# Attention, gated MoE and routed MoE in one kernel: conversions, router and sums of weights placed anew around the last tile

## The chip, the cores and the metric

The kernel runs on one core of a Trainium2 chip. The core has five engines with instruction queues of their own: TensorE (PE, with its weight load shown as PEld), VectorE (DVE), ScalarE (ACT), GpSimd (POOL) and SyncE (SP, which here only issues DMAs). The metric is the device time of one execution in microseconds, the median of several runs.

## The reference

Three layers follow each other. The output of the first is the input of the second, and so on:

```python
scores = scale * np.matmul(q, k.transpose(0, 1, 3, 2))     # 2 batches, 8 heads, 576 x 64
kth = np.partition(scores, -top_k, axis=-1)[..., -top_k:-top_k + 1]   # top_k = 32
scores = np.where(scores >= kth, scores, -1e9)
...                                                        # softmax, times v
xn = x / rms * rms_g                                       # 1152 tokens, 512 wide
...
(silu(xn @ w_gate) * (xn @ w_val)) @ w_out                 # d_ff 1536
...
logits = x @ w_gate                                        # 8 experts
expert_idx = np.argmax(logits, axis=1)
...                                                        # slots of an expert in token order, at most 288
h = np.maximum(np.einsum('ecd,edf->ecf', disp, w1), 0.0)   # w1: 8 x 512 x 1024
y = np.einsum('ecf,efd->ecd', h, w2)                       # w2: 8 x 1024 x 512
out[i] = gate_w[i] * y[expert_idx[i], pos[i]]
```

## The kernel before

Tokens are worked on in nine tiles of 128. While the attention of a tile runs, the dense MoE (moe1) and the routing (dispatch) of tiles before it are mixed in. The last tile, number 8, has nothing left to be mixed with; its work and that of the routed MoE's first expert lie from about 490 us on, and it is there that the change edits.

moe1 of a tile computes, for three groups g of 512 columns, the gate and value products (L502), the gating on VectorE (th at L511, gs at L514), a transposition on PE (turned, L486) and its split into two float16 halves (L471). Then come 36 matmuls into one output (L531), which ACT copies to yx (L535). dispatch transposes yx (xu, L546), computes the 8 router logits (L558), copies them (lg, L561), scales the row to two float16 halves (yh on ACT at L573, yl on DVE at L574), finds the best expert (m8, key, k8, the one-hot oh at L595), counts the tokens before it with two small matmuls (L598, L599, result read by scr at L606), computes the slot (L619) and scatters the row to its expert's place in DRAM (disp, L621).

The routed MoE's sixteen weights (w1 and w2 of 8 experts) are float32 in DRAM. Each is loaded into a raw buffer (L779, two halves), its squares are summed on ACT (L795), the sums go over PE (L806) into a scale by a few VectorE operations of one column (L807 to L816, with the shared helpers at L148 and L151), and it is then split into float16 halves, "high" on ACT (L825) and DVE (L827), "low" on DVE (L830). Weight number n counts in the order of loading; weights 2 and 3 are those which the diff calls convert(2, 2) and convert(3, 3).

Each expert's matmuls take 168 slots. Expert 0 is divided: block "a" of 128 slots that earlier tiles have mostly filled, and block "b" of 48 gathered after the last scatter (rest_gather, L906 to L912, an indirect DMA to xb and a transposing DMA to xbT). up multiplies by w1 (L925, three matmuls per product: high by high, high by low, low by high), takes the ReLU (L936 on ACT, L937 on DVE, called hE); down multiplies by w2 and scales (L945); send transposes back (L966), scales (L973) and scatters rows to the output (L1007). finish does this for the last expert, in two parts, with the last 128 columns of the result transposed at L997 into two buffers named col.

The order on each engine is written by a scheduler, which takes the instructions' dependences, priorities (tc.high_priority) and explicit constraints: after(t, "x") puts what is in its block behind the instruction that was noted as behind[t, "x"]. Accumulators for up and down come from the pool pacc, which has three buffers of one PSUM bank.

## Time and profile before

| | us |
|---|---|
| median of 3 runs | 660.68 (660.37 to 664.24) |
| the profiled execution | 663.15 |
| its span | 661.2 |
| PE busy | 588.5 (89%) |
| DVE busy | 540.5 (82%) |
| ACT busy | 502.3 (76%) |
| POOL busy | 353.8 (54%) |

All times of rows are those of the span of the profiled execution, which counts from its first instruction. Busy time is that in which an engine works; a releaser is what ended an idle time.

### The profile page before, as it was taken

What the parts mean: (1) busy time and instruction counts of PE and PEld (TensorE: products, weight loads), DVE (VectorE), ACT (ScalarE), POOL (GpSimd) and SP (SyncE); (2) the same over time, 40 slices, a digit from 0 to 9 for tenths busy, and PEclk for the clock granted to TensorE, in tenths of its full rate; (3) what the DMA queues carried; (4) which work ended last, traced back from release to release, by engine and by line L of the source; (5) the groups of instructions that cost most, each with busy time, mean ns of one, the idle gap of its engine ahead of it and who ended that gap; (6) DMA issues with size and microseconds to landing.
All of it is one profiled execution on the core that took longest, in us unless ns stands there. A gap on an engine that the chain in (4) does not pass through costs nothing.

```text
span 661.2 us, 13479 instructions
## 1 busy us (share of the span) xinstructions
PE 588.5 (89%) x4817; PEld 412.1 (62%) x4817; DVE 540.5 (82%) x1495; ACT 502.3 (76%) x972; POOL 353.8 (54%) x490
## 2 busy tenths in 40 slices
PE   1418879799999999999999999999998888999995
PEld 1314455545666666666666666665544688999995
DVE  3989999978989979989988999871379756999961
ACT  3459978997787878878897988875697539999721
POOL 2486644646468879958788688583212200123212
PEclk9999979799999999999999999999999898999998
DMA  8998355923000010100000000007600499999001
GB/s 217 271 327 292 142 183 181 303 85 83 20 16 25 18 45 9 33 17 29 14 13 30 17 26 0 1 17 266 245 17 34 142 213 395 309 355 359 28 22 43
DMA packets 47008, 80.07 MB, mean 121 GB/s; under 512 B 18717, under 2 KB 23325, under 8 KB 46931
## 3 DMA queue, kind: packets, MB, share of 16 engines
q1 hardware_dynamic: 45138, 74.28, 35.7%
q0 software_dynamic: 1792, 4.83, 2.0%
q8 instruction: 40, 0.66, 0.4%
q14 instruction: 38, 0.30, 0.1%
HBM read 64.35 MB, written 12.27 MB: 116 GB/s over the span
## 4 chain that ended last, share of the span: by engine, by line
PE 52%; DVE 17%; ACT 9%; DMA 8%; POOL 6%; issue 6%; SPq 1%; POOLq 0%; DVEq 0%; ACTq 0%
PE pm L502 15%; PE pm L531 9%; PE acc L925 7%; PE xps L430 6%; PE tp L317 5%; PE tp L422 4%; DVE split L830 3%; DMA vt<-in_v_l_dram 3%; DMA raw<-in_w_dram 3%; ACT junk L795 2%; DVE r L373 2%; DVE wbig L169 2%; DVE wbig L168 2%; PE pm L486 2%; DVE split L827 2%
## 5 line engine op out<-in xcount | busy, mean ns | idle before, releaser
L502 PE MATMUL pm<-wbig,xn 128*128 128x512 f16 x600 | 145.7, 379 | 0.5 <-DVE hT L471 0.5
L925 PEld LDWEIGHTS <-split 128*128 128x128 f16 x1728 | 116.4, 99 | 4.3 <-issue 2.0
L399 POOL TENSOR_TENSOR pp<-s,pp 128x576 f32<-128x576 f32 x72 | 101.9, 1431 | 21.8 <-ACT pp L398 21.5
L502 PEld LDWEIGHTS <-xn 128*128 128x128 f16 x648 | 62.3, 98 | 60.2 <-issue 0.9
L376 DVE MAX8 m<-r 128x8 f32<-128x288 f32 x216 | 96.5, 452 | 2.5
L373 DVE MATCH_REPLACE8 r<-m,r 128x288 f32<-128x288 f32 x216 | 95.1, 442 | 0.0
L317 PE MATMUL tp<-kst,qh 128*128 128x288 f32 (+1 forms) x160 | 64.9, 413 | 31.9 <-ACT s L319 14.6
L531 PE MATMUL pm<-wbig,hT 128*128 128x512 f16 x324 | 78.4, 386 | 0.0
L830 DVE SCALAR_TENSOR_TENSOR split<-raw,sc,split 128x2048 f16<-128x2048 f32 (+1 forms) x32 | 65.9, 2077 | 0.5 <-ACT split L825 0.5
L319 ACT ACTIVATE s<-tp 128x288 f32<-128x288 f32 x144 | 56.7, 416 | 11.1 <-PE tp L317 9.5
L423 ACT ACTIVATE pt<-tp 128x384 f32<-128x384 f32 x108 | 51.8, 499 | 15.2 <-PE tp L422 10.6
L317 PEld LDWEIGHTS tp<-kst,qh 128*128 128x128 f32 (+1 forms) x160 | 31.4, 197 | 50.5 <-ACT s L319 20.7
L422 PE MATMUL tp<-ident,pp 128*128 128x128 f32 x324 | 57.8, 288 | 5.3 <-DVE r L325 2.5
L430 PE MATMUL xps<-pt,vt 128*64 128x128 f32 (+1 forms) x800 | 62.4, 275 | 0.0
L925 PE MATMUL acc<-hE,split 128*128 128x168 f16 (+2 forms) x864 | 59.9, 231 | 1.7 <-DVE hE L937 1.7
L795 ACT ACTIVATE junk<-raw 128x2048 bf16<-128x2048 f32 (+1 forms) x32 | 54.1, 1692 | 6.9 <-DMA raw<-in_w_dram 6.7
L398 ACT ACTIVATE pp<-s,bias 128x576 f32<-128x576 f32 x72 | 52.2, 777 | 9.4 <-POOL bias L381 9.3
L404 ACT ACTIVATE pp<-pp,bias 128x576 f32<-128x576 f32 x72 | 57.0, 792 | 2.3 <-POOL pp L399 2.1
L925 PE MATMUL acc<-xgT,split 128*128 128x168 f16 (+1 forms) x768 | 58.0, 239 | 0.0
L422 PEld LDWEIGHTS tp<-ident,pp 128*128 128x128 f32 x324 | 40.5, 145 | 23.8 <-ACT pt L423 3.8
L430 PEld LDWEIGHTS xps<-pt,vt 128*64 128x64 f32 x800 | 43.9, 139 | 13.7 <-issue 12.0
L531 PEld LDWEIGHTS <-hT 128*128 128x128 f16 x324 | 30.4, 99 | 33.5 <-issue 2.7
(241 smaller groups left out, 1227.7 us busy)
## 6 DMA issues: line engine op xcount, KB each, us to landing
raw<-in_w_dram SPq DMA_DIRECT2D x28, 1024.0 KB, 7.4
wbig<-in_w_gate_dram SPq DMA_DIRECT2D x6, 1024.0 KB, 8.5
wbig<-in_w_val_dram SPq DMA_DIRECT2D x6, 1024.0 KB, 8.3
wraw<-in_w_out_dram SPq DMA_DIRECT2D x12, 512.0 KB, 5.8
disp<-wraw SPq DMA_DIRECT2D x18, 257.0 KB, 6.5
qraw<-in_q_l_dram SPq DMA_DIRECT2D x72, 64.0 KB, 2.2
wbig<-in_k_l_dram SPq DMA_DIRECT2D x16, 288.0 KB, 4.4
split<-in_w_dram SPq DMA_DIRECT2D x4, 1024.0 KB, 9.3
```

Source lines behind the costliest of these rows:

```text
L317: nc.tensor.matmul(sp[:c1], x[:, i, :c1], kst[b, hp][:, i, c * HALF:(c + 1) * HALF], start=(n == 0), stop=(n == 1))
L373: nc.vector.match_replace(h[i], to[n - 1][:, i], h[i], -3.0e38)
L376: nc.vector.max(to[n][:, i], h[i])
L399: nc.gpsimd.tensor_tensor(w, s[i], w, op=OP.subtract)
L404: nc.scalar.activation(pp[p][:, i], pp[p][:, i], AF.Exp, bias=bias[:, i, 0:1], scale=0.125, accum_out=sums[t][:, h:h + 1])
L422: nc.tensor.transpose(tp[:, i, :], p2[:, o:o + P], ident)
L430: nc.tensor.matmul(xps[t][rows, hp, c0:c1], v, w, start=(n == 0), stop=(n == 4))
L502: behind[t, "prod", b] = nc.tensor.matmul(a, xn[:, x + c, :], half(i, lo), start=(c == 0 and n == 0), stop=(c == KC - 1 and n == 2))
L531: nc.tensor.matmul(yps, hT[f // KC][:, KC * hi + f % KC, :], half(i, lo), start=(f == 0 and n == 0), stop=(f == NF1 - 1 and n == 2))
L795: nc.scalar.activation(junk, raw[:, g * 2 * BIG // k:(g + 1) * 2 * BIG // k], AF.Square, accum_out=sc[:, 9 + g:10 + g])
L830: nc.vector.scalar_tensor_tensor(lo[:, r], raw[:, r], sc[:, 7:8], hi[:, r], op0=OP.mult, op1=OP.subtract)
L925: nc.tensor.matmul(a, u[:, c, col * P:(col + 1) * P], v[:, c, :a.shape[-1]], start=(c == 0 and n == 0), stop=(c == nk - 1 and n == 2))
```

## The change

There are five edits. The low halves of weights 1, 2 and 3 get other places among the gates, the transposed tiles and the slot of the last tile. The router of the last tile goes ahead of the first 24 matmuls of up "a", and the low half yl moves behind the one-hot. The squares of a weight (squares) become a function apart from its sums and scale (scales); for weights 5 and 6 the sums are called one step later, and the call of ready() between up 1 and down "b" moves behind up 2's. The raw buffers of weights from 4 on are taken in the order 0, 2, 3, 1. pacc gets a fourth buffer, and the last two transposes of finish share one buffer.

```diff
@@ -555,7 +555,7 @@
         yield
         lp = px.tile([P, 3, E], F32, name="px")
         for c in range(KC):
-            nc.tensor.matmul(lp[:, 0, :], yT[:, c, :], rg[:, c, :], start=(c == 0), stop=(c == KC - 1))
+            behind[t, "lp"] = nc.tensor.matmul(lp[:, 0, :], yT[:, c, :], rg[:, c, :], start=(c == 0), stop=(c == KC - 1))
         yield
         lg = route.tile([P, E], F32, name="lg")
         nc.vector.tensor_copy(lg, lp[:, 0, :])
@@ -571,7 +571,6 @@
         nc.vector.tensor_scalar(yn[:, 5:6], yn[:, 1:2], YS, None, op0=OP.mult)
         if t == NT - 1:
             nc.scalar.activation(yh, y, AF.Copy, scale=yn[:, 5:6])
-            nc.vector.scalar_tensor_tensor(yl, y, yn[:, 5:6], yh, op0=OP.mult, op1=OP.subtract)
         else:
             nc.scalar.activation(y, y, AF.Copy, scale=yn[:, 5:6])
             nc.scalar.activation(yh, y, AF.Copy)
@@ -592,8 +591,10 @@
         yield
         oh = route.tile([P, E], BF16, name="oh")
         ev = nc.vector if t == NT - 1 else nc.gpsimd
-        ev.tensor_scalar(oh, rank8, k8[:, 0:1], None, op0=OP.is_equal)
+        behind[t, "oh"] = ev.tensor_scalar(oh, rank8, k8[:, 0:1], None, op0=OP.is_equal)
         if t == NT - 1:
+            with after(t, "oh"):
+                nc.vector.scalar_tensor_tensor(yl, y, yn[:, 5:6], yh, op0=OP.mult, op1=OP.subtract)
             nc.tensor.matmul(lp[:, 2, :], ones16, cum, start=True, stop=True)
         nc.tensor.matmul(lp[:, 1, :], before, oh, start=True, stop=False)
         behind[t, "pe"] = nc.tensor.matmul(lp[:, 1, :], ones16, cum, start=False, stop=True)
@@ -603,7 +604,7 @@
         ev.tensor_scalar(pos[:, 1:2], k8[:, 0:1], -float(cap), float(cap * E), op0=OP.mult, op1=OP.add)
         nc.vector.tensor_scalar(nm[:, 2:3], nm[:, 1:2], EPSD, None, op0=OP.add)
         yield
-        nc.vector.scalar_tensor_tensor(scr, lp[:, 1, :], 1.0, oh, op0=OP.mult, op1=OP.mult, accum_out=pos[:, 0:1])
+        behind[t, "scr"] = nc.vector.scalar_tensor_tensor(scr, lp[:, 1, :], 1.0, oh, op0=OP.mult, op1=OP.mult, accum_out=pos[:, 0:1])
         nc.vector.reciprocal(nm[:, 3:4], nm[:, 2:3])
         yield
         ev.tensor_scalar(pos[:, 2:3], pos[:, 0:1], float(cap), NOWHERE, op0=OP.is_ge, op1=OP.mult)
@@ -768,7 +769,7 @@
 
         if n < 2:
             return slots[2 + n]
-        return raws[n % 2 if n < 4 else n % 4]
+        return raws[n % 2 if n < 4 else (0, 2, 3, 1)[n % 4]]
 
     def load(j, n):
         e, w = divmod(j, 2)
@@ -782,8 +783,11 @@
     BIG = 4 * DM
 
     def size(j, n):
-
-        e, w = divmod(j, 2)
+        squares(j, n)
+        scales(j, n)
+
+    def squares(j, n):
+
         raw = raw_of(n)
         sc = ew.tile([P, 13], F32, name="sc", bufs=8)
         k = 4 if n < 4 or exact else 2
@@ -793,9 +797,11 @@
             else:
                 junk = ew.tile([P, BIG], BF16, name="junk")[:, :2 * BIG // k]
             nc.scalar.activation(junk, raw[:, g * 2 * BIG // k:(g + 1) * 2 * BIG // k], AF.Square, accum_out=sc[:, 9 + g:10 + g])
+        sized[j] = sc
+
+    def scales(j, n):
         with tc.high_priority(offset=4000) if n < 4 and not exact else nullcontext():
-            scale(e, w, n, k, sc)
-        sized[j] = sc
+            scale(*divmod(j, 2), n, 4 if n < 4 or exact else 2, sized[j])
 
     def scale(e, w, n, k, sc):
 
@@ -882,18 +888,20 @@
     with after(NT - 1, "xn"):
         convert(1, 1, True, (0, 1))
     with after(NT - 1, "gs", 0):
-        convert(1, 1, False, (2, 3))
-    with after(NT - 1, "th", 1), after(NT - 1, "tanh", 1):
+        convert(1, 1, False, (2,))
+    with after(NT - 1, "gs", 1):
+        convert(1, 1, False, (3,))
+    with after(NT - 1, "th", 2), after(NT - 1, "tanh", 1):
         convert(2, 2, True, ())
-    with after(NT - 1, "gs", 1):
+    with after(NT - 1, "gs", 2), after(NT - 2, "scr"):
         convert(2, 2, False, (0, 1))
     with after(NT - 1, "dve"):
         convert(2, 2, False, (2, 3))
     fetch_w()
     size(3, 3)
-    pacc = ctx.enter_context(tc.tile_pool(name="pacc", bufs=3, space=PSUM, reuse_waits="tile"))
+    pacc = ctx.enter_context(tc.tile_pool(name="pacc", bufs=4, space=PSUM, reuse_waits="tile"))
     pback = ctx.enter_context(tc.tile_pool(name="pback", bufs=2, space=PSUM, reuse_waits="tile"))
-    ptp = ctx.enter_context(tc.tile_pool(name="ptp", bufs=2, space=PSUM, side="right", reuse_waits="tile"))
+    ptp = ctx.enter_context(tc.tile_pool(name="ptp", bufs=1, space=PSUM, side="right", reuse_waits="tile"))
     held = []
     if not exact:
         held.append(tc.alloc_tile_pool(name="held", bufs=1, side="right"))
@@ -930,11 +938,11 @@
         for lo, hi in groups(NF2, n):
             a = pacc.tile([P, hi - lo, n], F32, name="acc")
             for c in range(lo, hi):
-                with nullcontext() if early is None or c < early else after(NT - 1, "pe"):
+                with nullcontext() if early is None else after(NT - 1, "lp" if c < early else "pe"):
                     product(a[:, c - lo, :], place(2 * e), (xgT[k][:, :KC], xgT[k][:, KC:]), KC, F2, c)
             hh, hl = (x[:, lo:hi, :] for x in hE[k])
             nc.scalar.activation(hh, a, AF.Relu)
-            nc.vector.scalar_tensor_tensor(hl, a, 0.0, hh, op0=OP.max, op1=OP.subtract)
+            behind[k, "up"] = nc.vector.scalar_tensor_tensor(hl, a, 0.0, hh, op0=OP.max, op1=OP.subtract)
 
     def down(k, e, n):
         yT2[k] = eb.tile([P, KC, n], F32, name="yT2", bufs=1)
@@ -992,8 +1000,9 @@
         with tc.issue_after(last.ins):
             product(z[:, 0, :], place(2 * k + 1), hE[k], NF2, DM, x, range(cut, NF2))
         nc.vector.tensor_scalar(y[:, x:, :], z, es[k][:, 8:9], None, op0=OP.mult)
+        cols = ptp.tile([P, 2, P], F32, name="col")
         for i, (o, m) in enumerate(chunks(W)):
-            tp = ptp.tile([P, P], F32, name="col")
+            tp = cols[:, i, :]
             nc.tensor.transpose(tp[:m], y[:, x, o:o + m], ident)
             scaled(i, held[1 + i][1][:, x * P:], tp[:m], meta[k, i][:m, 0:1])
 
@@ -1012,9 +1021,11 @@
 
     up("a", 0, WA, 2)
     with after(NT - 1, "dve"), after(NT - 1, "tanh", 2):
-        convert(3, 3, True, (0, 1))
+        convert(3, 3, True, (0,))
     with after(NT - 1, "slot"), after(NT - 1, "gate"):
-        convert(3, 3, False, (2, 3))
+        convert(3, 3, False, (1, 2))
+    with after("a", "up"):
+        convert(3, 3, False, (3,))
     last = gather(1, 1, 0, W, eb, nc.sync)
     rest_gather()
     notes(1, 1, 0, W, eb, nc.sync)
@@ -1034,8 +1045,10 @@
         if n == 4:
             with after(NT - 1, "act"):
                 size(ORDER[4], 4)
+        if 5 <= n <= 6:
+            scales(ORDER[n], n)
         if n + 1 < 2 * E:
-            size(ORDER[n + 1], n + 1)
+            (squares if n < 6 else size)(ORDER[n + 1], n + 1)
         convert(ORDER[n], n)
         fetch_w()
 
@@ -1044,7 +1057,6 @@
     ready()
     send("a", WA, True)
     up(1, 1, W)
-    ready()
     down("b", 0, WB)
     ready()
     cnt = pback.tile([P, DM], F32, name="back")
@@ -1064,6 +1076,8 @@
         up(e, e, W)
         if done[0] < 2 * E - 1:
             ready()
+            if e == 2:
+                ready()
         if e == 2:
             send("b", WB, True)
         else:
```

Three places in the order show what the scheduler makes of it. Names carry the number of their tile; split2 and split3 are the destinations of weights 2 and 3, raw0 the raw buffer of weight 2.

VectorE, around the last tile's gate of group 2 (gs_6141, of th_6099), before:

```order
L511 SCALAR_TENSOR_TENSOR th_6099<-th_6099,late_6100 128x512
L830 SCALAR_TENSOR_TENSOR split2_5991<-raw0_5993,sc_6304,split2_5991 128x1024 x2
L514 SCALAR_TENSOR_TENSOR gs_6141<-late_6128,st_79,th_6099 128x512
L471 TENSOR_TENSOR hT_6006<-pm_6104,hT_6006 128x512
L604 TENSOR_SCALAR nm_6024<-nm_6024 128x1
L807 TENSOR_SCALAR sc_6342<-st_5988 128x1
L606 SCALAR_TENSOR_TENSOR scr_6069,pos_6068<-px_5961,oh_6047 128x8
L607 RECIPROCAL nm_6024<-nm_6024 128x1
L809 TENSOR_SCALAR sc_6342<-sc_6342 128x1
L810 TENSOR_SCALAR sc_6342<-sc_6342 128x1
L148 TENSOR_SCALAR sc_6342<-sc_6342 128x1
```

and now:

```order
L471 TENSOR_TENSOR hT_6006<-pm_6104,hT_6006 128x512
L514 SCALAR_TENSOR_TENSOR gs_6141<-late_6128,st_79,th_6099 128x512
L605 TENSOR_SCALAR nm_6024<-nm_6024 128x1
L813 TENSOR_SCALAR sc_6342<-st_5988 128x1
L607 SCALAR_TENSOR_TENSOR scr_6069,pos_6068<-px_5961,oh_6047 128x8
L836 SCALAR_TENSOR_TENSOR split2_5991<-raw0_5993,sc_6304,split2_5991 128x1024 x2
L608 RECIPROCAL nm_6024<-nm_6024 128x1
L815 TENSOR_SCALAR sc_6342<-sc_6342 128x1
L471 TENSOR_TENSOR hT_6007<-pm_6150,hT_6007 128x512
L836 SCALAR_TENSOR_TENSOR split2_5991<-raw0_5993,sc_6304,split2_5991 128x1024 x2
L816 TENSOR_SCALAR sc_6342<-sc_6342 128x1
L148 TENSOR_SCALAR sc_6342<-sc_6342 128x1
```

The two low halves of weight 2 (L830, now L836) stand behind the gate rather than ahead of it, and the exponent of weight 3 (the rows of sc_6342, ending in L148) comes behind four low halves.

PE, from the sums of weight 4 (st_5988) in down "a" (acc_6516, operands hE0 and hE1), before:

```order
L806 LDWEIGHTS ones16_70
L806 MATMUL st_5988<-s16_6720,ones16_70 128x1 [waits DVE_49]
L806 LDWEIGHTS ones16_70
L806 MATMUL st_5988<-s16_6720,ones16_70 128x1
L925 LDWEIGHTS split1_5990
L925 MATMUL acc_6516<-hE0_6381,split1_5990 128x128 [waits Activation_49]
L925 LDWEIGHTS split1_5990
L925 MATMUL acc_6516<-hE1_6382,split1_5990 128x128 [waits DVE_49]
```

and now:

```order
L812 LDWEIGHTS ones16_70
L812 MATMUL st_5988<-s16_6720,ones16_70 128x1
L812 LDWEIGHTS ones16_70
L812 MATMUL st_5988<-s16_6720,ones16_70 128x1
L933 LDWEIGHTS split1_5990
L933 MATMUL acc_6516<-hE0_6381,split1_5990 128x128 [waits Activation_49]
L933 LDWEIGHTS split0_5989
L933 MATMUL acc_6616<-xbT_6499,split0_5989 128x48 [waits DMAHW6_49]
```

One matmul of down "a" follows the sums in both; then the products of up "b" (xbT_6499) come, of which the first waits for a DMA, and the other 83 of down "a" stand behind 42 of them.

PE, its last matmuls, which end in the two transposes to col (yT2_8574 is the result to be transposed), before:

```order
L925 LDWEIGHTS split0_5989
L925 MATMUL acc_8576<-hE0_8326,split0_5989 128x168
L997 MATMUL col_8691<-ident_64,yT2_8574 128x128 [waits DVE_49]
L997 MATMUL col_8694<-ident_64,yT2_8574 40x128
L1076 TENSOR_LOAD top_7017 [waits DVE_49]
L53 COMPARE_AND_BRANCH
```

and now:

```order
L933 LDWEIGHTS split0_5989
L933 MATMUL acc_8576<-hE0_8326,split0_5989 128x168
L1006 MATMUL col_8691<-ident_64,yT2_8574 128x128 [waits DVE_49]
L1006 MATMUL col_8691<-ident_64,yT2_8574 40x128 [waits Activation_49]
L1090 TENSOR_LOAD top_6987 [waits DVE_49]
L53 COMPARE_AND_BRANCH
```

The second transpose goes to the same tile as the first and waits for ACT, which reads that one.

## Rows read from the trace of the kernel before

**Rows 1.** Stretches of the span: start:end, length, busy us (instructions), clock, DMA share, GB/s.
```profile
510.75:513.50 2.75, 2.75 (x8) 0.91 (x6) 2.55 (x10) 2.70 (x3) 2.13 (x4) 0.50 0.87 354
...
536.05:537.74 1.69, 0.01 (x2) 0.01 (x1) 1.69 (x1) 0.00 (x0) 0.00 (x0) 1.00 0.49 102
551.30:554.36 3.06, 3.06 (x86) 3.06 (x83) 2.99 (x13) 3.06 (x4) 0.00 (x0) 0.53 1.03 420
554.36:620.99 66.63, 66.63 (x918) 66.32 (x915) 64.00 (x110) 62.83 (x68) 13.81 (x7) 1.00 0.94 302
```

**Rows 2.** Timeline of DVE: start, duration, operation, tile, [idle before, its releaser].
```profile
506.86 2.46 DVE L830 SCALAR_TENSOR_TENSOR split<-raw,sc,split 128x1024 f16<-128x1024 f32 x2
509.25 0.73 DVE L514 SCALAR_TENSOR_TENSOR gs<-late,st,th 128x512 f32<-128x512 f32 x1
...
511.14 0.15 DVE L148 TENSOR_SCALAR sc<-sc 128x1 int32<-128x1 int32 x1
...
524.74 0.27 DVE L619 TENSOR_SCALAR slot<-pos 128x1 int32<-128x1 f32 x1
...
625.64 4.60 DVE L830 SCALAR_TENSOR_TENSOR split<-raw,sc,split 128x2048 f16<-128x2048 f32 x2
...
654.65 0.34 DVE L1002 TENSOR_SCALAR last<-col,notes 40x128 f32<-40x128 f32 x1 [0.54 <-PE col L997]
```

**Rows 3.** Timeline of PE, columns as in rows 2.
```profile
510.04 0.72 PE L486 MATMUL pm<-ident,gs 128*128 128x128 f32 x4 [1.82 <-DVE gs L514]
...
520.13 1.50 PE L925 MATMUL acc<-xgT,split 128*128 128x128 f16 x24
521.47 1.01 PE L558 MATMUL px<-rg,xu 128*128 128x8 f32 x8
...
531.26 4.79 PE L925 MATMUL acc<-hE,split 128*128 128x128 f16 x83 [0.51 <-DVE hE L937]
537.74 2.60 PE L925 MATMUL acc<-xbT,split 128*128 128x48 f16 x96 [1.68 <-DMA xbT<-xb]
...
549.87 0.19 PE L806 MATMUL st<-s,ones 128*128 128x1 bf16 x2 [2.94 <-DVE s L804]
...
550.86 3.67 PE L925 MATMUL acc<-hE,split 128*128 128x48 f16 x96
...
623.25 7.12 PE L925 MATMUL acc<-hE,split 128*128 128x168 f16 x96 [1.23 <-DVE hE L937]
630.21 7.12 PE L925 MATMUL acc<-xgT,split 128*128 128x168 f16 x96
...
654.17 0.44 PE L997 MATMUL col<-ident,yT 128*128 128x128 f32 x2 [0.49 <-DVE yT L994]
```

**Rows 4.** The chain of waits: start, duration, engine and line.
```profile
510.76 8.11 PE pm L531 x30
...
518.89 0.70 ACT yx L535
...
522.18 0.75 DVE yd L574
```

**Rows 5.** Timeline of ACT, columns as in rows 2.
```profile
511.32 2.19 ACT L825 ACTIVATE split<-raw,sc 128x1024 f16<-128x1024 f32 x2
...
520.33 0.60 ACT L546 ACTIVATE xu<-px 128x512 f32<-128x512 f32 x1
...
654.54 0.37 ACT L1004 ACTIVATE last<-col,notes 128x128 f32<-128x128 f32 x1 [1.22 <-PE col L997]
```

**Rows 6.** Timeline of POOL, columns as in rows 2.
```profile
525.88 1.27 POOL L621 DMA_INDIRECT disp<-yd,slot  x1 [1.40 <-DVE slot L619]
...
657.01 0.93 POOL L1007 DMA_INDIRECT out_dram<-last,to  x1 [0.31 <-issue]
```

**Rows 7.** Timeline of SP's DMA queue, columns as in rows 2.
```profile
518.18 0.38 SPq L779 DMA_DIRECT2D raw<-in_w_dram  x1
```

**Rows 8.** DMA issues of the page: line, count, KB each, median us to landing.
```profile
raw<-in_w_dram SPq DMA_DIRECT2D x28, 1024.0 KB, 7.4
```


## The prediction

> **What bounds the kernel now.** The page's busy shares put PE first, but they are an average, so I read stretches. The table of stretches shows the routed experts from 554.36 to 620.99: PE busy 66.63 of 66.63 us, DVE 64.00, ACT 62.83, DMA engines at 0.94 [rows 1]. All four are nearly full there; only an earlier start, or fewer stops of PE, shortens that stage. The two views that follow, the chain of waits and the timelines, are read for how this start comes about. In the chain, the last tile of the dense MoE runs from VectorE's gating into the transposes, the 30 output products, ACT's yx, and the router with its long row of small VectorE operations [rows 2 to 5]; it ends in the slot number and the last scatter of tokens [rows 6]. From that scatter hang the gather of block "b", its transposition and 96 products at 537.74, which waited 1.68 us for it [rows 3]. Thirdly PE's own stops: 2.94 us at 549.87 (sums of a weight's squares), 1.23 us before 623.25 [rows 3].
>
> **The last tile: VectorE's low halves.** Two low halves of weight 2, 2.46 us, stand before the gate of group 2 and now follow it [rows 2]. This is on the chain: the gate starts at 509.25 and PE, after 1.82 us of idling, turns its result at 510.04 [rows 2, 3]. So the turn comes 2.46 us earlier. The products behind it ran at a granted clock of 0.50 for 2.75 us from 510.75 [rows 1]; less idling ahead of them may leave the clock at 1.00, which saves half of that, 1.4 us (bounds 0 and 1.4). I take it, since the low half moved out of PE's preceding wait as well; the products, 8.11 us in the chain [rows 4], would end 3.9 us earlier.
>
> ACT does not allow that whole gain. Its pair of conversions of weight 3 (2.19 us at 511.32 [rows 5]) stands ahead of yx in its order and waits for an exponent that VectorE wrote at 511.14 [rows 2]. That write now comes behind four low halves (twice 2.46 us [rows 2]) and a halving of a transposed tile: gate at 506.8, its end at 507.5, plus 4.9, plus some 1.3 of small operations (0.15 each, as the exponent itself) and one of about the gate's 0.73: 513.7. ACT's pair then ends at 515.9, and yx, at 518.89 before [rows 4], starts there: 3.0 us earlier. This replaces the 3.9.
>
> **The router.** The 24 early products of "a" started at 520.13 and lasted 1.50 us; the transposed row was ready at 520.33 + 0.60 = 520.93, yet the router started at 521.47 [rows 3, 5]. With the router ahead it saves 0.54. The logits' copy then waited for VectorE's low half of y, 0.75 us at 522.18 [rows 4], till 522.93, with the router done at 521.47 + 1.01 = 522.48 [rows 3]: 0.45 more. This low half now stands between the one-hot and the slot: 0.75 back. The 24 products come after instead; they delay "a", which has idle time behind it. Sum to the slot (524.74) and the scatter (525.88) [rows 2, 6]: -3.0 - 0.54 - 0.45 + 0.75 = **-3.2 us**. Ends: -2.3, if the clock's part fails, and -4.4, if ACT's pair is ready early.
>
> **PE behind the scatter.** Before, 83 products of down "a", 4.79 us at 531.26, ran while "b" was on its way [rows 3]. The scheduler now puts 42 products of up "b" ahead of them, and the first of these waits for the transposing DMA, as the order shows. Everything behind it on PE waits too: the 83 products, the rest of up "b", up 1. So the 4.79 us move from under the wait to behind it. PE then idles for about 6 us (528.5 to 534.5) rather than 1.68. What the clock does then is bounded by rows: after the 1.69 us stretch 536.05 to 537.74 it stayed at 1.00, and after the 2.94 us stop it fell to 0.53 for 3.06 us [rows 1, 3]. I take 1.4 us lost (half of 2.75), with ends 0 and 2.8. The stop of 2.94 us goes, because the sums' matmuls now stand behind down "b", where VectorE's inputs are long there. With it goes the half clock in down "b": 96 products took 3.67 us there, and the same number and shape in up "b" 2.60 [rows 3]; 1.07 off. Sum: +4.79 + 1.4 - 1.07 - 2.94 = **+2.2 us**.
>
> On the clock, the trace has both cases, no drop after 1.69 us and a drop after 2.94. The Trainium skill, "TensorE: Matmul & The Clock Gate", section "What's actually happening", says that the throttled state is the default and that activity releases it; by this the long wait would surely cost a slow start, and the sum would keep its 1.4. Were the short stop's row to decide, the sum would be 1.4 lower. The 2.94 us row is nearer to a 6 us wait, and by it the page's rule holds here.
>
> **The fourth accumulator.** The 1.23 us ahead of 623.25 were spent waiting for VectorE's hE to free one of three buffers [rows 3]; a fourth takes it away: **-1.23**, ends -1.23 and 0. What would be late next is weight 14: its last two low halves, 4.60 us from 625.64, end at 630.24, just as PE began up 7 at 630.21 [rows 2, 3]. They must come earlier too; the loads' start moves with the scatter, and VectorE has 2.63 us of idle time in the stage [rows 1].
>
> **The last columns.** Two transposes took 0.44 us together at 654.17 [rows 3]. They now share a buffer, and the second waits for ACT's copy, 0.37 us at 654.54 [rows 5]; this delays VectorE's scaling at 654.65 by about 0.5 [rows 2]. But the store that needs it went out at 657.01, 2.0 us after that scaling ended, behind the store before it [rows 2, 6]. So 0; if that cover were gone, up to 0.8.
>
> **The rest at nothing.** Squares are computed apart from sums, in ACT's queue, which has 3.8 us of room over the stage; the raw buffers change places in the loads' order, under DMA at 0.94 [rows 1]. On SP the second half of weight 4 now goes ahead of the gather of "a" and its notes, where it was issued at 518.18 after them [rows 7]; that is a rival's ground.
>
> **Sum.** -3.2 + 2.2 - 1.23 + 0 = -2.2 us (-3.2 + 2.18 - 1.23 = -2.25). The profiled execution took 663.15 us, 2.5 over the median of 660.68; the sum is taken off the median: **658.4 us**. Its ends: -4.4 + 0.78 - 1.23 = -4.85, or 655.8; and -2.3 + 3.58 + 0 + 0.8 = +2.1, or 662.8.
>
> **Rivals.**
> *Full gain.* PE's clock does not fall after the long wait, and ACT's pair does not hold yx. For it: the 1.69 us row; against it: the 2.94 us one. It gives 655.8. A step further, "b" arrives before PE has run out of work, and the 4.79 and 1.4 fall away too, leaving -1.07 - 2.94 = -4.0 behind the scatter: 660.68 - 4.4 - 4.0 - 1.23 = 651.0; for that "b" would have to come 9 us earlier, and nothing in the rows speaks for it.
> *The scatter waits (slower side).* The last scatter writes rows that the gather of "a" and its notes must have read. A load of 1024 KB landed after 7.4 us in the median [rows 8], and the gather now queues behind one. With the load out at about 514 the gather could land at 523 or later, where the scatter is due at 522.7. From that point on each microsecond is lost; by 3.2 us later the whole gain of the tile is gone: 660.68 + 2.2 - 1.23 = 661.6, and with one more half-clock stretch of 1.4, 663.0. Against it: the transfers of 510.75 to 513.50 ran at 354 GB/s [rows 1], by which 1024 KB take 3.0 us.
> *VectorE holds the end.* Weight 14's low halves don't follow, since hE comes from a PE that is only 1.0 us earlier after the scatter. Then the stop at 623 turns into a wait at 630: 660.68 - 1.0 = 659.7.
> *Nothing.* PE's 83 products go behind the wait and eat all of the tile's gain, and weight 14 holds the rest: 660.7, at the edge of the last.
>
> **Chances.** Forecast 0.5, full gain 0.15, scatter 0.17, VectorE or nothing 0.18. The forecast's own range is 655.8 to 662.8; 655.3 to 663.0 leaves out the tails of the first two rivals, and some 0.2 in all. One per cent, 6.6 us, is about what a measurement of this kernel can tell from no change: faster means under 654.1, slower over 667.3. The first needs a full gain in which the wait for "b" costs nothing; the second more than one rival at once. Faster 0.10, same 0.85, slower 0.05.
>
> **What would show it.** The gate of group 2 starts at about 506.8, yx at 516, the slot at 521.5; PE idles some 6 us before the first product on xbT at 534.5, and the 83 products of down "a" follow it; no stop of 2.9 us before the sums, none of 1.2 us after up 6; the final store goes out when the one before it is issued. If yx comes at 515.0, ACT's wait was wrong; if the scatter starts over 1.5 us after its slot, the load was in the way; if PE stops before up 7, weight 14 holds it. The forecast falls if the slot comes less than 2 us earlier, or if PE does not idle before xbT.

## The result and the profile after

The changed kernel takes 667.42 us (median of 8 runs, 666.04 to 669.25); the kernel before, run beside it, 662.5 us (8 runs, 658.46 to 664.64). The ratio is 1.009 with a 95% interval of 1.0066 to 1.0115: **the change costs about 4.9 us, 0.9%**, where 658.4 us were forecast, 2.2 us under the time before, and above the stated range of 655.3 to 663.0. The prediction had put the border of "slower" at one per cent, or 667.3 us; the ratio lies just under it, the time just over it. The profiled execution took 666.40 us, with a span of 664.4 us.

The first 480 us are the same program, yet their length differs by execution. So times are also given from a marker: the start of the last tile's first transposes of the attention's output (L465), up to which the order is the same in all kernels here. It is at 478.63 in the trace before and at 477.30 in that after.

The stretches after; columns as in [rows 1]:

```profile
507.45:514.20 6.75, 6.64 (x32) 2.84 (x29) 6.68 (x12) 1.90 (x3) 4.47 (x4) 1.00 0.49 183
...
527.50:532.33 4.83, 0.00 (x1) 0.00 (x0) 4.66 (x9) 2.00 (x1) 0.00 (x0) 0.68 0.83 142
532.33:539.62 7.29, 7.29 (x125) 7.29 (x125) 3.47 (x2) 0.60 (x1) 0.00 (x0) 0.74 1.03 334
...
550.91:604.00 53.09, 53.09 (x735) 52.92 (x731) 50.24 (x92) 45.70 (x49) 6.57 (x5) 1.00 1.04 321
604.00:624.28 20.28, 15.63 (x196) 15.07 (x195) 16.14 (x28) 16.55 (x20) 1.92 (x2) 0.93 0.37 118
```

The 30 products of the last tile run at a clock of 1.00, where [rows 1] has 0.50 for 2.75 us. Then PE stands still from 527.50 to 532.33, and its clock is 0.74 in the 7.29 us behind. Up to 604.00 PE is full. In the next 20.28 us it works 15.63.

PE's timeline after; columns as in [rows 3]:

```profile
477.30 0.64 PE L465 MATMUL xps<-ident,x 128*128 128x128 f32 x4
...
506.96 0.66 PE L486 MATMUL pm<-ident,gs 128*128 128x128 f32 x4 [0.88 <-DVE nm L605]
507.45 6.64 PE L531 MATMUL pm<-wbig,hT 128*128 128x512 f16 x30
...
532.33 1.84 PE L933 MATMUL acc<-xbT,split 128*128 128x48 f16 x42 [4.84 <-DMA xbT<-xb]
533.99 5.79 PE L933 MATMUL acc<-hE,split 128*128 128x128 f16 x83
...
548.38 2.59 PE L933 MATMUL acc<-hE,split 128*128 128x48 f16 x96
550.81 0.19 PE L812 MATMUL st<-s,ones 128*128 128x1 bf16 x2
...
607.60 0.19 PE L812 MATMUL st<-s,ones 128*128 128x1 bf16 x2 [0.91 <-DVE s L810]
...
621.45 0.19 PE L812 MATMUL st<-s,ones 128*128 128x1 bf16 x2 [3.73 <-DVE s L810]
621.50 1.28 PE L933 MATMUL acc<-xgT,split 128*128 128x168 f16 x8
622.57 1.91 PE L974 MATMUL back<-ident,yT 128*128 128x128 f32 x8
624.28 7.41 PE L933 MATMUL acc<-hE,split 128*128 128x168 f16 x96
...
656.38 0.29 PE L1006 MATMUL col<-ident,yT 128*40 128x128 f32 x1 [0.46 <-ACT last L1013]
```

The row at 532.33 is the wait that the order showed, with the 83 products behind it. The 2.94 us stop ahead of down "b" [rows 3] is gone; the sums of weight 5 now come behind down "b", at 550.81. The 1.23 us stop of [rows 3] is gone too, but two others are there, 0.91 and 3.73 us, both at sums of squares, and the matmuls behind the longer one run slow (8 transposes 1.91 us; at 602.16 they took 1.04).

DVE's timeline; columns as in [rows 2]:

```profile
506.17 0.74 DVE L514 SCALAR_TENSOR_TENSOR gs<-late,st,th 128x512 f32<-128x512 f32 x1
...
512.71 0.15 DVE L148 TENSOR_SCALAR sc<-sc 128x1 int32<-128x1 int32 x1
...
520.69 0.26 DVE L620 TENSOR_SCALAR slot<-pos 128x1 int32<-128x1 f32 x1
...
552.48 1.28 DVE L833 TENSOR_SCALAR split<-raw,sc 128x2048 f16<-128x2048 f32 x1
...
605.06 2.34 DVE L836 SCALAR_TENSOR_TENSOR split<-raw,sc,split 128x2048 f16<-128x2048 f32 x1
...
621.22 0.17 DVE L810 CAST s<-sc 128x2 bf16<-128x2 f32 x1 [3.80 <-ACT junk L799]
```

ACT's timeline; columns as in [rows 5]:

```profile
512.90 2.19 ACT L831 ACTIVATE split<-raw,sc 128x1024 f16<-128x1024 f32 x2 [4.65 <-DVE sc L148]
514.99 0.67 ACT L535 ACTIVATE yx<-pm,st 128x512 f32<-128x512 f32 x1
...
539.02 1.91 ACT L799 ACTIVATE junk<-raw 128x2048 bf16<-128x2048 f32 x1 [7.21 <-DMA raw<-in_w_dram]
...
541.59 1.91 ACT L799 ACTIVATE junk<-raw 128x2048 bf16<-128x2048 f32 x1
...
617.15 1.91 ACT L799 ACTIVATE junk<-raw 128x2048 bf16<-128x2048 f32 x1 [3.69 <-SPq L53]
```

And the view of the raw buffers' instructions between 590 and 622 us (count, ns as min/median/max, first and last start; then the time from issue to landing):

```profile
L780 SPq DMA_DIRECT2D raw<-in_w_dram x5: 367/368/533, 591.0 to 607.4; - x5
...
DMA to landing us min/median/max: 9.6/9.6/9.6
```

The long stop can be followed back through these three. PE waits for DVE's cast at 621.22, that for ACT's squares, the last of which start at 617.15 and 619.19; their load was issued at 607.40, when DVE's low half that read the raw buffer had ended (605.06 + 2.34), and landed 9.6 us later. This is the last weight, number 15. The squares of weight 5, in contrast, were done at 543.5, and its conversion started only at 552.48, behind sums that PE did at 550.81.

POOL's last rows; columns as in [rows 6]:

```profile
521.81 1.26 POOL L622 DMA_INDIRECT disp<-yd,slot  x1 [1.57 <-ACT junk L799]
...
658.42 0.93 POOL L1016 DMA_INDIRECT out_dram<-last,to  x1 [0.30 <-issue]
```

The last store follows the one before it, so the wait between the two column transposes cost nothing.

### The profile page after: what moved, and what is told of

It reads as the page before. It is cut to its first block, busy times and chain, and to the rows that moved or that the text cites. A ratio compares the mean times of both kernels' runs of the same rounds, so it can differ in the third digit from the quotient of the medians.

```text
span 664.4 us, 13481 instructions
## 1 busy us (share of the span) xinstructions
PE 589.2 (89%) x4817; PEld 413.4 (62%) x4817; DVE 540.3 (81%) x1495; ACT 502.6 (76%) x972; POOL 353.7 (53%) x490
## 5 line engine op out<-in xcount | busy, mean ns | idle before, releaser
L531 PE MATMUL pm<-wbig,hT 128*128 128x512 f16 x324 | 76.6, 380 | 0.0
L836 DVE SCALAR_TENSOR_TENSOR split<-raw,sc,split 128x2048 f16<-128x2048 f32 (+1 forms) x32 | 65.8, 2077 | 0.1
L531 PEld LDWEIGHTS <-hT 128*128 128x128 f16 x324 | 30.2, 98 | 32.4 <-issue 0.9
```

The costliest lines, as they stand in the source:

```text
L531: nc.tensor.matmul(yps, hT[f // KC][:, KC * hi + f % KC, :], half(i, lo), start=(f == 0 and n == 0), stop=(f == NF1 - 1 and n == 2))
L836: nc.vector.scalar_tensor_tensor(lo[:, r], raw[:, r], sc[:, 7:8], hi[:, r], op0=OP.mult, op1=OP.subtract)
```

## The experiments

The change was taken apart, then one reason after the other was put to the test. In the tables, slot, xbT (the first product of "b"), up 2 and the last group (the last matmuls of down 7) are in us from the marker, read from one trace each. "Stops" are PE's from up 2 on.

| kernel | slot | xbT | up 2 | last group | stops | ratio to before (95%) |
|---|---|---|---|---|---|---|
| before | 46.1 | 59.1 | 75.7 | 174.2 | 1.23 | 1 |
| change | 43.4 | 55.0 | 73.6 | 177.0 | 0.91, 3.73 | 1.0090 (1.0066 to 1.0115) |
| e5, fourth buffer alone | 44.4 | 56.5 | 74.7 | 176.0 | 0.92, 3.36 | 1.0113 (1.0084 to 1.0143) |
| e3, change with three buffers | 45.0 | 57.6 | 70.1 | 173.7 | 3.40 | 1.0034 (1.0007 to 1.0060) |
| e1, change with sums back | 43.4 | 55.6 | 73.9 | 177.8 | 1.79, 3.35 | 1.0048 (1.0018 to 1.0077) |
| e4, last tile's edits alone | 45.3 | 57.7 | 71.5 | 172.8 | 1.82, 0.78, 1.25 | 1.0011 (0.9982 to 1.0040) |
| e8, change, "b" behind "a" | 43.4 | 56.8 | 69.1 | 173.3 | 0.27, 2.78, 0.35, 0.42 | 1.0005 (0.9981 to 1.0030) |
| e11, e8 with sums back | 43.4 | 56.5 | 75.8 | 172.5 | none | 0.9999 (0.9974 to 1.0025) |

**e3_three_acc** takes the fourth buffer out of the change:

```diff
-    pacc = ctx.enter_context(tc.tile_pool(name="pacc", bufs=4, ...
+    pacc = ctx.enter_context(tc.tile_pool(name="pacc", bufs=3, ...
-        cols = ptp.tile([P, 2, P], F32, name="col")
-            tp = cols[:, i, :]
+            tp = ptp.tile([P, P], F32, name="col")
```

> The change without its fourth accumulator and the shared column buffer (pacc 3, two column buffers). In the order the 83 products of down a stand ahead of those of up b again, and weights 8 and 9 are converted one after the other. Theory RING (the time is lost because the low halves of weights 8 and 9 are interleaved, which frees a raw buffer some 2.3 us late, so that the last weights' loads and sums come late and PE stops 3.7 us in up 6): that stop is gone, up 2 starts at about 545 to 546, and the kernel is 8 to 9 us faster than the changed one, about 3 us faster than the kernel before (ratio 0.995). Theory BOUND (loads and VectorE's conversions set the end whatever comes before up 2): up 2 starts as early, but PE stops elsewhere before up 7, and the time is that of the kernel before within 1 us. Theory PLACE (the 83 products behind the wait are the loss): the loss of 4.8 and of the slow clock goes, but a stop in up 6 of over 2 us stays.

**e5_four_acc_alone** makes the same edit the other way round in the kernel before.

> The kernel before with only the fourth accumulator and the shared column buffer. 32 products of up b now stand ahead of 83 of down a. Theory PLACE: PE waits some 7 us before the first product on xbT instead of 1.7, up 2 starts 4 to 5 us later than 554.4, and the end is 3 to 5 us later than before (the 1.2 us stop goes). Theory BOUND: the later start is absorbed since weights come no later, within 1 us of before. Theory RING: weights 8 and 9 are not interleaved, so no stop of 3.7 us in up 6; the time is PLACE's.

By itself the fourth buffer costs 1.13%, and without it the change is 0.56% better than with it (1.0034 and 1.0090, their intervals just apart): it is the edit that costs most. The interval of e3 lies above 1 too, so some 0.3% may belong to the other edits. With the buffer alone the scheduler already places 32 products of "b" ahead of 83 of down "a". PE's timeline of e5:

```profile
536.42 1.44 PE L925 MATMUL acc<-xbT,split 128*128 128x48 f16 x32 [3.66 <-DMA xbT<-xb]
537.68 5.62 PE L925 MATMUL acc<-hE,split 128*128 128x128 f16 x83
...
629.83 3.65 PE L925 MATMUL acc<-hE,split 128*128 128x168 f16 x48 [3.36 <-DVE hE L937]
```

The stop for hE, which the buffer was to take away, is there in another form, 48 products into the same product: hE is late because VectorE is.

**e1_sums_back** undoes the edits on sums and ready():

```diff
-        if 5 <= n <= 6:
-            scales(ORDER[n], n)
-            (squares if n < 6 else size)(ORDER[n + 1], n + 1)
+            size(ORDER[n + 1], n + 1)
...
+    ready()
     down("b", 0, WB)
...
-            if e == 2:
-                ready()
```

> The change with the sums of weights 5 and 6 and the calls of ready() put back. Weights 8 and 9 are converted one after the other; the 42 products of up b still stand ahead of the 83 of down a. Theory RING: the stop of 3.7 us in up 6 is gone, so the time is 3 to 5 us under the changed kernel's, about 663; a stop of up to 3 us for the sums of weight 5 is back before up 2. Theory BOUND: as the changed kernel within 1 us. Theory PLACE: as the changed kernel, the long wait before xbT unchanged at about 4.8 us.

Weight 5's conversion starts at 69.7 us from the marker, not 75.2, yet the last group comes at 177.8. The wait for xbT is 5.68 us here. The ratio's interval overlaps that of the change.

**e4_last_tile_alone** undoes that edit too, the buffers' order and the fourth buffer; what is left are the edits of the last tile.

> The kernel before with only the edits of the last tile (low halves, router, yl): raw buffers, sums and accumulators as before. PE order has the 83 products ahead of up b. Theory RING: slot 4 us earlier, up 2 at about 549 to 550, no interleaving, so 3 to 4 us faster than before (ratio 0.994 to 0.996). Theory BOUND: up 2 earlier by as much, but stops before up 7 make it the time of before within 1 us.

Up 2 starts 4.2 us earlier from the marker, the last group 1.4, and the time is the same within 0.4%. The earlier start is real; it does not arrive.

**e8_b_behind_a** is the change, all of it, with one constraint that puts up "b" behind down "a" again:

```diff
-                with nullcontext() if early is None else after(NT - 1, "lp" if c < early else "pe"):
+                with (after("a", "dpe") if k == "b" else nullcontext()) if early is None else after(...):
...
-                product(a[:, c - lo, :], place(2 * e + 1), hE[k], NF2, DM, c)
+                behind[k, "dpe"] = product(a[:, c - lo, :], place(2 * e + 1), hE[k], NF2, DM, c)
```

> The whole change, with one constraint more: the products of up b stand behind all products of down a on PE, as in the kernel before. Theory CONVERSIONS (from weight 5 on VectorE converts one weight after the other at about 8 us each, slower than PE uses them, so the end is set by when weight 5's conversion starts; in the change it waits for sums that stand behind down b on PE): the wait for xbT falls to about 2 us, up 2 starts 4 to 6 us earlier than in the change (counted from the last tile's first transposes), weight 5's conversion starts as much earlier, and the end comes 4 to 6 us earlier, at the kernel before or 1 us under it. Theory LATE STOP (the change's loss arises only behind up 2, from the late load of weight 15 and its sums ahead of up 6's last matmuls): the stop of 3.7 us stays or grows, the time is the changed kernel's within 1 us.

It is level with before (1.0005), and its interval lies wholly under that of the change: one constraint on PE's order takes the loss back, with the fourth buffer still there. It does not act on PE alone, though: from the conversion of weight 4 on, 31 of VectorE's 158 instructions stand in another order in e8's trace than in that of the change (in the two traces of the change, 2). PE's timeline of e8:

```profile
530.72 4.79 PE L933 MATMUL acc<-hE,split 128*128 128x128 f16 x83 [0.51 <-DVE hE L946]
535.72 2.58 PE L933 MATMUL acc<-xbT,split 128*128 128x48 f16 x96 [0.21 <-DMA xbT<-xb]
...
547.97 0.19 PE L812 MATMUL st<-s,ones 128*128 128x1 bf16 x2
...
561.79 0.19 PE L812 MATMUL st<-s,ones 128*128 128x1 bf16 x2 [2.78 <-DVE sc L813]
561.84 7.09 PE L933 MATMUL acc<-hE,split 128*128 128x168 f16 x56
```

The wait for xbT falls from 4.84 to 0.21 us, and the 83 products take 4.79 rather than 5.79. Up 2 starts 6.6 us before that of the kernel before. Behind it PE stops 2.78 us, 56 products then take 7.09 us where 96 take 7.12 at full clock, and of 6.6 us 0.9 are left.

**e11_b_behind_a_sums_back** is e8 and e1 together.

> As the run before it, and the sums of weights 5 and 6 and the calls of ready() put back too, so that the sums of weight 5 stand in up 1. CONVERSIONS: weight 5's conversion starts another 2 to 3 us earlier; the end comes at 3 us under the kernel before unless the order on VectorE puts hE behind a conversion, as it did in the change with the sums back (a stop of 3.4 us in down 6), which gives the time of before. LATE STOP: like the change with the sums back, 3 us over the kernel before.

PE never stops from up 2 on, but 5.12 us in up 1, for weight 5. PE, and ACT, in e11:

```profile
546.00 0.19 PE L812 MATMUL st<-s,ones 128*128 128x1 bf16 x2 [5.12 <-DVE s L810]
```

```profile
543.74 1.91 ACT L799 ACTIVATE junk<-raw 128x2048 bf16<-128x2048 f32 x1 [1.48 <-DMA raw<-in_w_dram]
```

ACT squares the second half of weight 5 as soon as the load lands, so here the stop hangs on a load; the DMA engines' share was 1.01 from 541 to 546 us. What the last tile gains, PE spends waiting for weight 5.

**e10_last_tile_raw_order** is e4 with the new order of the raw buffers, 1.0014 (0.9989 to 1.0038), against 1.0011 for e4: the order of the buffers alone is worth nothing that shows.

> The kernel before with the last tile's edits and the new order of raw buffers, three accumulators and the sums where they were. CONVERSIONS: against the last tile's edits alone the sums of weight 5 come some 1 to 2 us earlier where the loads do; the order puts them behind up 1, so weight 5's conversion starts when down b does, no earlier than about 71 us behind the last tile's first transposes; the end is within 1 us of that kernel's. LATE STOP: weight 15 is loaded into the buffer of weight 11, as in the change, so a stop of 2 to 4 us in up 6 appears.

**e9_extra_low_half** adds 2.34 us to VectorE in the kernel before, by computing one low half of weight 7 twice:

```diff
+            for _ in range(2 if n == 7 and g == 0 else 1):
                 nc.vector.scalar_tensor_tensor(lo[:, r], raw[:, r], ...
```

> The kernel before with one low half of weight 7 computed twice: 2.3 us more of VectorE's work, nothing else added. CONVERSIONS: weight 14's conversion, which PE waits for at up 7 with no slack, moves by 2.3 us and so does the end: 2 to 2.5 us slower than before. If PE sets the pace (weight 5 is ready 10 us ahead of its use), no change within 0.5 us.

1.0066 (1.0026 to 1.0106), that is 4.4 us (1.7 to 7.0): the interval holds the 2.34 us, so VectorE's time in the routed stage can be paid for at the end in full, and the middle is nearly twice that. In the trace up 2 starts at 75.4 us from the marker and the last group at 177.9, 3.7 later than before, with stops of 0.60, 0.45, 1.18 and 2.53 us, the last three for hE (that up 7 waits for weight 14, as expected here, is a wrong reading; the next section has it). The test is not clean: the second computation also holds weight 7's raw buffer longer, and from the conversion of weight 4 on the scheduler put 32 of some 160 instructions of VectorE in another order.

VectorE's conversions follow each other at 7.9 us per weight in the trace before (that of weight 5 starts 73.5 us from the marker, that of weight 15 at 152.7). PE takes 96.8 us from up 2 to the last group where it does not stop (e11), for 13 products by a weight, 7.4 us each. Over ten weights that is 5 us that PE would gain on VectorE. VectorE's pace is not fixed, however: by the same reckoning it is 7.6 us in e4 and 8.3 in the change.

These paces do not say what PE stops for. In none of the traces of the kernels above does a stop behind up 2 wait for a converted weight. The rows name VectorE's short instructions (casts of sums, scales, hE, yT), which stand in its queue between the halves of weights, and once ACT's hE (e10, 2.51 us).

**VectorE relieved by POOL.** Three kernels let POOL compute the second high half of weights from 5 on: e13 on e11, e14 on the kernel before, and e15, for weights 6, 8, 10, 12, 13 and 14 alone, on e8.

```diff
-                nc.vector.tensor_scalar(hi[:, r], raw[:, r], sc[:, 7:8], None, op0=OP.mult)
+                (nc.gpsimd if n >= 5 and not exact else nc.vector).tensor_scalar(hi[:, r], raw[:, r], ...
```

> The change with up b behind down a and the sums back, and besides with the second high half of each weight from number 5 on (1.28 us on VectorE each) computed by POOL. CONVERSIONS: VectorE has 11 x 1.28 = 14 us less to do, so the conversions keep ahead of PE as long as POOL's half (estimated at 5 us from its 1.43 us for 576 columns) does not hold the low halves; PE's stops behind up 2 go, and the end comes 2 to 5 us under the kernel before. LATE STOP (loads and sums, not VectorE, hold PE): no better than that kernel without POOL, the time of before.

> The kernel before with the same high halves on POOL and nothing else. CONVERSIONS: PE's stop of 1.2 us at 623 goes and nothing else can, since PE had no other stop behind up 2: 1 to 1.5 us faster, or nothing if POOL's halves are late. If VectorE slows down beside POOL (its low halves longer than 2.34 us), slower.

> The change with up b behind down a, the sums where the change has them, and six of the high halves (weights 6, 8, 10, 12, 13, 14) on POOL. CONVERSIONS: 7.7 us of VectorE's work less; the end comes 1 to 3 us under the kernel before; up 2 is not stopped by the sums of weight 5. LATE STOP: as that kernel without POOL, the time of before within 1 us.

All three are much slower: 1.0341 (1.0301 to 1.0381), 1.0352 (1.0309 to 1.0396) and 1.0414 (1.0375 to 1.0452). They did not take load off VectorE: its busy time is 556.7, 561.3 and 561.5 us, where the kernels that they are built on have 541.5, 540.5 and 539.5. The last section has the rows. As tests of what VectorE's relief would bring they decide nothing.

**Weight 5 earlier.** Since e11 waits for weight 5's load, five kernels issue it earlier: e16 (on e11), e17 (the same with three buffers) and e18 (on e8) behind the notes of "a"; e19 (on e11) and e20 (three buffers, without the constraint on "b") behind the transposing DMA of "b", and the gathers of experts 2 and 3 behind that load.

```diff
+    with after("a", "notes"):          # e19, e20: after("xb"), further down
+        fetch_w()
     last = gather(1, 1, 0, W, eb, nc.sync)
...
-        for _ in range(3):
+        for _ in range(2):
             fetch_w()
```

> As the change with up b behind down a and the sums back, and the load of weight 5 issued right behind the notes of a (about 518) instead of behind the gathers (about 532). CONVERSIONS: weight 5 lands before 527, its sums stand in down a, its conversion starts some 55 to 60 us behind the last tile's first transposes instead of 70, the stop of 5.1 us for the sums in up 1 goes, and the end comes 3 to 5 us earlier than in that kernel, ratio to before 0.993 to 0.996. LATE STOP: the end stays, ratio 1.000. If the load delays the last scatter or the gather of b on the DMA queues, up 2 starts 2 to 3 us later and eats half of the gain.

> The same with three accumulators and two column buffers. CONVERSIONS: as the run before it, within 1.5 us, with up to 1.3 us of stops for an accumulator; the fourth accumulator's own worth is the difference.

> The whole change with up b behind down a, and weight 5 loaded behind the notes of a; the sums where the change has them by its calls. CONVERSIONS: weight 5 is converted before 65 us behind the last tile's first transposes, and the end is 2 to 5 us under that kernel's, ratio to before 0.993 to 0.997. LATE STOP: 1.000.

> The change with up b behind down a and the sums back, with weight 5's load put behind the transposition of b and ahead of the gathers of experts 2 and 3 (which then land later). TWO CHAINS (the end is the later of PE's work behind up 2, 96.8 us without a stop, and of VectorE's conversions, about 98 us from weight 5): weight 5's sums come in up 1 with a stop of under 2 us instead of 5.1, up 2 starts at 70 to 73 us and weight 5's conversion at 63 to 67 us behind the last tile's first transposes, and the end comes 2 to 4 us earlier than in that kernel, ratio to before 0.994 to 0.997. RING (loads of the last weights hold it, through four raw buffers): up 2 and weight 5 early as said, but stops of 3 us in up 6 or down 6, ratio 1.000.

> The same with three accumulators (PE's order then has up b behind down a by itself). TWO CHAINS: as the run before it within 1.5 us; ratio 0.994 to 0.999. RING: 1.000 or above.

| kernel | conversion of weight 5 starts | xbT | up 2 | last group | ratio to before (95%) |
|---|---|---|---|---|---|
| e16 | 63.6 | 61.0 | 74.1 | 172.4 | 0.9987 (0.9965 to 1.0009) |
| e17 | 64.4 | 59.0 | 77.2 | 176.4 | 1.0034 (1.0013 to 1.0055) |
| e18 | 68.1 | 59.9 | 74.7 | 177.7 | 1.0049 (1.0017 to 1.0082) |
| e19 | 68.2 | 55.6 | 74.3 | 174.2 | 1.0033 (1.0003 to 1.0064) |
| e20 | 69.4 | 56.8 | 76.0 | 178.1 | 1.0066 (1.0037 to 1.0096) |

In e16 the stop in up 1 is gone, but "b" pays for it. POOL's timeline of e16:

```profile
526.29 1.26 POOL L622 DMA_INDIRECT disp<-yd,slot  x1 [1.57 <-ACT junk L799]
532.34 0.97 POOL L916 DMA_INDIRECT xb<-disp,rest  x1 [4.79 <-DMA disp<-yd,slot]
```

The gather waits 4.79 us for the scatter to land, in the change 2.14; the load is in its way, and xbT comes 4.5 us later than in e11. In e19, which keeps the load out of its way, the stop in up 1 remains (4.78 us). None is faster than before: e16's interval holds 1.

A theory of mine on the way, that the start of weight 5's conversion sets the end, fell here: it varies from 63.6 to 75.6 us among these kernels, and the last group does not follow (172.4 with 63.6, 177.7 with 68.1, 173.3 with 75.6 in e8). A second one, that the late load of weight 15 by itself is the loss, is not borne out either: e8 keeps the buffers' order and both edits of ready(), and that stop is gone with the place of "b".

**b2_before_again** and **a2_change_again** are the two kernels once more, for a second trace of each.

> The kernel before once more, for a second profile of the same program. If the stretch up to the last tile's first transposes (478.6 us in the first profile; 477.1 to 483.6 in the kernels run so far, which have the same order there) varies from execution to execution, it differs from 478.6 by up to some us while the stretch behind it takes 182.6 within 1 us; if it belongs to a program, both are repeated within 0.5 us.

> The changed kernel once more. If its loss belongs to the order of its instructions, the wait for xbT (4.8 us), the start of weight 5's conversion (75.2 us behind the last tile's first transposes) and a stop of 3 to 4 us for the sums of weight 15 in up 6 come again, each within 0.7 us. If it belongs to that one execution, the stop is under 2 us here.

The change repeats itself: up 2 at 74.2, last group at 177.7, stops of 1.50 and 3.10 us. The kernel before does not quite. PE's timeline of its second trace:

```profile
538.50 3.75 PE L925 MATMUL acc<-xbT,split 128*128 128x48 f16 x96 [1.85 <-DMA xbT<-xb]
...
549.93 0.19 PE L806 MATMUL st<-s,ones 128*128 128x1 bf16 x2 [0.94 <-DVE s L804]
...
623.90 7.12 PE L925 MATMUL acc<-hE,split 128*128 128x168 f16 x96 [1.36 <-DVE hE L937]
```

The same program waits 0.94 us for weight 5's sums, where [rows 3] has 2.94; up 2 starts at 73.0, 2.8 earlier, and the last group at 173.2, 1.0 earlier. With no edit at all, about a third of an earlier start arrived.

## Why the prediction was wrong

Up to the first product of up 2 the steps came as forecast in kind, and not far off in size; the sum failed behind it. From the marker:

| stretch | before | after | difference | forecast |
|---|---|---|---|---|
| marker to slot | 46.1 | 43.4 | -2.7 | -3.2 |
| slot to up 2 | 29.6 | 30.2 | +0.6 | +2.2 |
| up 2 to the last group | 98.5 | 103.4 | +4.9 | -1.23 |
| last group to the end | 8.4 | 10.1 | +1.7 | 0 |
| sum | 182.6 | 187.1 | +4.5 | -2.2 |

The sum of 4.5 us agrees with the medians (4.9). The last row is not the column wait: the last store goes out 4.1 us after the last group in both, and the span then ends 6.0 us after it, before 4.2, in the change's second trace 4.4.

**The last tile: right.** The times of the forecast count in the trace before, whose marker lies 1.33 us later, so they are compared from the marker: the gate came 1.75 us earlier (forecast 2.46), yx 2.57 (forecast 3.0) and the slot 2.7 (forecast 3.2). The products behind the gate ran at full clock, and ACT's pair held yx: it started when the exponent came, at 512.71, and yx at 514.99 followed at once. By the prediction's own sign, a yx at 515.0 would have made ACT's wait wrong; counted from the marker this one stands at 516.3. "ACT does not allow that whole gain" is what the trace shows.

**PE behind the scatter: right in kind.** PE idled 4.84 us before xbT (forecast about 6), with the 83 products behind. The half clock cost 1.00 on the 83 products and 0.7 on the 42 (1.84, against 42/96 of 2.60): 1.7, forecast 1.4. The Trainium skill, "TensorE: Matmul & The Clock Gate", section "What's actually happening", says that the throttled state is the default; on this wait the trace agrees, with a clock of 0.74 behind it. The stop of 2.94 and the slow down "b" went (2.59 us, not 3.67). The stretch was 1.6 better than forecast, mostly as "b" landed 10.5 us after its scatter's issue instead of 11.9. But e8 shows what this order cost: without it up 2 comes 4.5 us earlier still, and the change is level with before.

**The step that failed: "The fourth accumulator", with "The rest at nothing".** The text said that a fourth buffer takes 1.23 us away; by itself it costs 1.13%, some 7.5 us (e5). It also said that weight 14's low halves "must come earlier too"; in the change that weight's conversion starts at 628.07, 150.8 us from the marker, 5.2 later than before. The reason given was a wrong reading: the low halves ended at 630.24 just as PE began up 7, but up 7 does not use them. By the kernel's list of the loads (ORDER) up 7 multiplies by weight 13, and weight 14 is used by down 6, which in PE's timeline of the kernel before is this row, 7.8 us later:

```profile
638.04 7.12 PE L925 MATMUL acc<-hE,split 128*128 128x168 f16 x96
```

The sum also booked each microsecond gained or lost ahead of up 2 one for one at the end, and credited the sums' new place with the whole 2.94 us. The runs showed another thing: the start of up 2 does not set the end. Behind it PE (7.4 us per weight where it does not stop) and VectorE (7.9 in the trace before) go at nearly one pace, and a load waits until VectorE has freed its buffer, as weight 15's did at 607.40. So a start gained ahead is mostly given back as a stop, in up 1 (e11), in down 1 (e8, e3) or in up 6 (the change). e4 is the clean case: 4.2 us earlier at up 2, nothing measured at the end.

Nor does the loss of the change arise as the sum would have it. Its up 2 starts 2.1 us earlier than that of the kernel before, and its last group comes 2.8 later; the time goes in the stops of 0.91 and 3.73 us and the slow matmuls behind them. And e11 starts up 2 1.9 us later than e1, from which it differs by the constraint alone, yet has its last group 5.3 earlier. So the plus terms of the sum were not simply carried to the end either: +4.79 and +1.4 are 6.2, and the 5.6 us (0.85%) between e8 and the change lie near that, but between e11 and e1 it is 3.2 us (0.49%), and the agreement may be luck. What is shown is that the order with the products of "b" ahead of the 83 costs, and that the fourth buffer brings it; not how it comes to the late stops, since VectorE's order changes with it.

Moving the sums was no gain of 2.94 us either. Weight 5's conversion started at 75.2 rather than 73.5, later though the tile was earlier, because its sums wait behind down "b" for 7 us with their squares done. That puts the stop at another place; e8 against e11 (1.0005 and 0.9999) says that it costs or brings nothing that shows where "b" stands behind; in the change's order it may cost some 0.4% (1.0090 against e1's 1.0048, intervals overlapping).

**"VectorE holds the end"** was nearest in kind, since nearly all stops behind up 2 wait for VectorE; but it rested on weight 14 at up 7, and its sign, a stop ahead of up 7, did not come. "Nothing", at 660.7, is what e4, e8 and e11 show, the kernels without the order that the fourth buffer brings. No rival priced a loss from that buffer. "The scatter waits" did not come: the scatter was issued 0.86 us after its slot ended.

**Left open.** In three kernels the measured loss is larger than the trace's last group tells (e5: +7.5 us by the ratio, +1.8 by the trace; e3: +2.3 and -0.5; e19: +2.2 and 0.0). The traced execution of e5, 666.51 us, was the fastest of its five, whose median is 669.8; the first 480 us differ by several us between executions, and one trace each can't settle it. Nor is it settled which of VectorE, a load or the buffers starts each stop in the routed stage; the scheduler gives VectorE and ACT another order in each kernel. No run keeps VectorE's order and moves the 83 products alone, so their place and VectorE's order that comes with it are not told apart. That the stop at weight 15 in the change comes from weights 8 and 9 having their low halves mixed, which frees a buffer late, is read from one order; e1 converts them one after the other and loses that stop, but has another of 3.35 us for hE in its place.

## What to carry to other kernels

Before a gain ahead of a balanced stage is added to the sum, ask which engine or queue in that stage has room to keep it; where they go at nearly one pace, count the gain at nothing until a trace shows otherwise. A loss there is not read off from the start of the stage either: look at the stops inside it. Two rows that meet in time are no dependence; look up in the kernel which product uses the weight. A larger pool is also an edit of the order: look at what the scheduler now starts early, and at which DMA its first instruction waits for, with what behind it. Where an edit costs, one constraint that restores the old order, with the resource kept, tells order and resource apart; compare the other engines' orders too, as the scheduler may move them along.

## What the runs showed of the hardware

**POOL and VectorE in each other's way.** In e14 POOL took 5.44 to 7.55 us for a high half that takes 1.28 on VectorE, and VectorE's low halves beside it grew. DVE and POOL in e14:

```profile
566.88 3.83 DVE L830 SCALAR_TENSOR_TENSOR split<-raw,sc,split 128x2048 f16<-128x2048 f32 x1
...
581.17 6.56 DVE L830 SCALAR_TENSOR_TENSOR split<-raw,sc,split 128x2048 f16<-128x2048 f32 x1
```

```profile
564.80 11.22 POOL L827 TENSOR_SCALAR split<-raw,sc 128x2048 f16<-128x2048 f32 x2
...
581.84 5.47 POOL L827 TENSOR_SCALAR split<-raw,sc 128x2048 f16<-128x2048 f32 x1
```

The low half at 581.17 lasts until 587.73, just past POOL's 587.31; over the kernel the mean of 24 rose from 2.34 to 3.36 us, which is more than the 11 halves saved (24.3 us against 14.0). The Trainium skill, "SBUF — State Buffer", section "SBUF: two separate sides", has VectorE's operations on two SBUF inputs and GpSimd share a pair of ports that the one that starts first holds for a whole instruction. The low half has two such inputs, and the rows agree that the two hold each other up; they do not agree on the order, for the low half at 581.17 began 0.67 us before POOL's and still took 6.56 us, though spans on POOL are rough. In e15 the six high halves that stayed on VectorE beside POOL's took 4.24 us in the mean.

**The clock behind a short wait is not the same each time.** After 1.69 us of waiting for xbT the 96 products took 2.60 us [rows 3], at a granted clock of 1.00; in the second trace of the same program, after 1.85 us, they took 3.75, at a granted clock of 0.57, so most of them at the half clock.
